# Which keys of a fused attention and feed-forward kernel the SP queue loads, and a new written-out order of its operations

## The chip, the cores and the metric

The kernel runs on one core of a Trainium2 chip. A core has five engines that run side by side and wait for one another by semaphores: TensorE (PE in the profile; PEld is its loading of weights), VectorE (DVE), ScalarE (ACT), GpSimd (POOL) and SyncE (SP), and 16 DMA engines that move data between the main memory (DRAM) and the on-chip memory. A DMA is issued by an instruction in the queue of SP, ACT or POOL. The metric is the device time of one execution in microseconds (us).

## The reference

```python
# attention: q, k, v are [4 batches, 8 heads, 768 tokens, 64] float32
scores = (q @ k.transpose) / sqrt(64)
keep   = (key position < 4) | (0 <= token - key position < 128)     # 4 sinks and a window of 128
a      = softmax(where(keep, scores, -1e9))
x      = (a @ v), heads side by side: [3072 tokens, 512]
# feed-forward: w_in [512, 2048], w_out [2048, 512]
h      = x @ w_in
out    = (h * sigmoid(1.702 * h)) @ w_out                            # [3072, 512] float32
```

## The kernel before

**Tiling.** The 3072 tokens are 24 blocks of 128 tokens, 6 for each batch. The list `ORDER` (0, 6, 12, 18, 1, 2, 3, ...) says in which order the blocks are worked on; the text calls the place of a block in it its position p0 to p23. Positions 0 to 3 are the first blocks of the four batches (block 0, 6, 12, 18). Because the window is as long as a block, a block needs the keys and values of itself and of the block before it, and the four sinks. Two positions make a group: g0 is p0 and p1, up to g11.

**Attention of one block.** Its q and its k are loaded as fp16 into a buffer `qkn` (a ring of 4, one for each group). They are transposed into `qkt`: for p0 to p7 by TensorE (`t_qk`, w0 for q and w1 for k, lines 420 and 427) with a copy out of PSUM by ACT or DVE (`copy_qk`), later by a transposing DMA of SP (line 455). Then come the scores (`scores`, line 503; `masks`, line 495, for p0 to p3), on DVE the packing of both halves (549), the maximum (559, 570 to 579) and its subtraction (600, 624), on ACT the exponential (639), the transposition of the weights `a` into `at` (TensorE, line 679, up to p5; then a DMA of SP, line 704), two selections on POOL (642, 646), the product with the values (`values`, lines 731, 737, 741), the normalization on DVE (`norm`, 748 and 749) into `xn`, and the transposition of `xn` into `xt` (TensorE, line 767, up to p5; then one DMA of SP for each group, line 780).

**Feed-forward of one group.** 8 operations `first` (line 802) make `h` transposed, ACT or ACT with DVE apply the gate into `gt` (832, 816, 823), and 8 operations `second` (line 856; t0 and t1 for the two blocks, n0 to n3 for quarters of the contraction) make the output, which is copied out of PSUM (`osb`, 377 or 381) and stored (874). `first` and `second` of an earlier group stand in TensorE's queue between the attention of later blocks. PSUM buffers of the ring `mm` (3) serve the transpositions, `first` and `second`.

**Loads.** POOL issues the loads that change the type from fp32 to fp16 on the way: q and k of p0 to p3 in large pieces (line 299), the others in small ones (306), the values (277), four parts of w_in (315, here i0 to i3) and four of w_out (324, o0 to o3). One load goes another way: the blocks named by `CFG["hw"]` are loaded as fp32 by SP into a tile `raw`, and one of three engines rounds it into `qkn`:

```python
got = plan.add({SP: 0.45, ACT: 0.6}, -120 + n, 0, lambda e, ...: by(e).dma_start(raw, src), ...)      # line 284
return plan.add({DVE: 0.42, ACT: 0.6, POOL: 0.8}, -110 + n, 0, round16, deps=[got], take=[buf])       # line 295
```

**The order.** Every operation is put on a list by `plan.add` and has its number there. What is issued, in which order and on which engine, is read from the string `SEQUENCE` alone: `37s` is operation 37 on SP, and the letters p, a, d, t, s stand for PE, ACT, DVE, POOL and SP. The costs given to `plan.add` (0.57 and the like) are not used by `run`:

```python
for word in SEQUENCE.split():                                                                         # line 142
    op = self.ops[int(word[:-1])]
    op.on = {"p": PE, "a": ACT, "d": DVE, "t": POOL, "s": SP}[word[-1]]
```

Each engine works its own operations off in this order, and a later one never passes an earlier one of the same engine or queue. Which buffer of a ring an operation gets follows from the order too.

Of the kernel before, what the change touches and what calls it, by code (L numbers as in the profile page):

```python
# [27 lines left out]
PE, ACT, DVE, POOL, SP = "PE", "ACT", "DVE", "POOL", "SP"  # L28
# [30 lines left out]
126p 8d 125a 26t 149p 109d 127a 147p 21t 129p 110d 148a 130p 23t 111d 150a 2d 112a 131d 33t 114p 113a 133d 172p 116p  # L59
115a 105t 132d 152p 135a 117d 120p 30t 173a 134d 170p 118p 137p 121d 29t 136a 153p 119d 139p 138a 122p 171a 141p  # L60
154d 24t 140a 175p 155d 143p 156d 123a 176p 151t 157d 144d 481p 142d 158a 34t 484p 482a 177d 145p 9d 159a 483d 146a
160p 180d 485a 161d 27t 182a 487p 486d 488a 178d 128t 493p 162p 489d 494a 163d 28t 495d 490p 179d 166p 164p 40t 491a
167d 478p 183p 492d 39t 181a 165d 479a 32t 184d 499p 185p 187p 480d 36t 500a 186d 195p 193p 189p 501d 43t 194a 188d
496p 196a 217p 31t 190d 215p 168p 497a 197p 169a 498d 191p 218a 216a 199d 514p 198p 42t 192a 508p 200d 201d 518p
515a 519a 509p 35t 202d 239p 203d 237p 48t 219p 220p 240a 238a 54t 502p 221d 503p 222d 520p 204a 223d 46t 504p 224d
225d 510p 5d 241p 93s 226a 49t 1s 511p 45t 512d 505p 242p 521a 73t 516p 243d 506a 44t 517a 524p 205p 244d 41t 525a
245d 528p 206d 247d 529a 522p 253p 255p 246d 523a 254d 530p 256d 61t 208p 227p 209d 257p 97d 207t 248a 531p 270s
230p 228a 259d 210t 231a 532p 258p 260d 211p 229t 261d 526p 249s 212d 263d 232t 533p 233p 52t 262d 527a 536p 55t
234d 213p 214d 57t 537p 271p 51t 264a 534a 538p 235p 273d 265s 236a 539p 272p 250t 274d 540a 548p 275d 53t 277d 552p
62t 276d 550p 549a 283p 296s 553a 554p 284p 285d 555a 266t 542p 94s 551a 286d 251p 59t 287d 544p 47t 252d 545a 289d  # L70
546p 58t 543a 267p 547a 50t 288d 558p 268d 564p 297p 278a 269s 556p 513s 298p 299d 565p 279s 300d 559p 541s 557a
301d 507s 98t 566p 95s 302d 60t 303d 578p 290a 567p 309p 568d 304a 291s 560p 311d 576p 280t 305s 579a 312d 561p 577a
281p 562a 310p 570p 282d 322s 313d 571a 572p 292t 574p 314d 315d 535s 575a 65t 580p 293p 581a 66t 573a 584p 294d
585a 586p 306t 295s 592p 74t 587p 316a 90t 582p 64t 307p 317s 69t 593p 308d 583a 67t 588p 323p 63t 604p 70t 325d
605a 589p 324p 56t 590a 326d 594p 79t 327d 612p 72t 328d 613a 600p 335p 601a 595p 318t 337d 329d 596a 606p 174t 607a
348s 598p 338d 602p 336p 603a 339d 608p 341d 599a 319p 609a 340d 620p 320d 614p 330a 610p 321s 615p 342a 361p 621p
343s 362p 611a 363d 563s 622p 591s 364d 616p 365d 331s 638p 366d 639a 617p 367d 374s 618a 623p 344t 349p 75t 632p
597s 351d 569s 633a 628p 350p 624a 352d 634p 332t 353d 345p 635a 355d 84t 629a 630p 346d 68t 631a 636p 88t 626p 85t
333p 627a 637a 91t 640p 334d 78t 641a 648p 354d 99t 347s 642p 81t 649p 375p 76t 356a 650p 377d 368a 643p 376p 357s
378d 651p 379d 369s 644p 380d 668p 625s 652d 387p 619s 645p 389d 669a 656p 400s 646d 657a 660p 358t 390d 381d 658p  # L80
659a 662p 370t 359p 663a 83t 654p 360d 77t 655a 664p 388p 661a 71t 371p 391d 665a 82t 666p 372d 670p 392d 393d 382a
373s 676p 401p 394a 383s 671p 403d 677p 402p 667a 395s 404d 678p 405d 647s 407d 672p 96s 679p 406d 680d 673p 413p
384t 674d 684p 408a 415d 696p 385p 409s 414p 416d 396t 685a 686p 386d 687a 426s 690p 397p 691a 697a 692p 398d 693a
688p 417d 419d 410t 689a 399s 682p 86t 418d 411p 683a 80t 694p 412d 87t 695a 698p 427p 100t 699p 429d 420a 710p 430d
700p 428p 421s 431d 701p 681s 711a 702a 716p 432d 724p 452s 439p 725a 717a 675s 718p 703s 441d 433d 719a 712p 422t
713a 714p 442d 440p 715a 443d 720p 423p 721a 732p 424d 704p 444d 434a 445d 722p 733p 446a 435s 705p 653s 734p 723a
425s 465p 706p 466p 447s 467d 726p 468d 735p 436t 469d 471d 736a 707p 437p 708a 470d 709s 727p 438d 746p 448t 747a
742p 89t 449p 743a 92t 728p 450d 738p 472a 451s 729p 737s 453p 730d 744p 739a 473s 455d 745a 752p 456d 750p 751a
740p 454p 741a 457d 772p 459d 753a 773a 748p 458d 749a 778p 474t 779a 760p 768p 761p 460a 770p 762p 461s 475p 771a
763p 769a 476d 764a 766p 767a 774p 775a 776p 777a 782p 462t 783p 780p 781a 788p 784p 463p 789p 464d 754p 477s 790p  # L90
731s 785p 786d 791p 792d 755p 796p 797a 756p 802p 803a 757p 758d 806p 759s 807a 808p 793s 809a 787s 794p 765s 795a
798p 799a 800p 822p 801a 804p 823p 805a 810p 824p 811p 825p 826d 816p 827a 812p 817p 813p 818p 828p 814a 819p 829p
815s 830p 820d 831p 832a 821s 833a
"""


# [69 lines left out]
def kernel(  # L166
# [224 lines left out]
    o_qkt, o_ks, o_own_s, o_x = {}, {}, {}, {}  # L391

    for p, b in enumerate(ORDER):
        bb, r = divmod(b, 6)
        g, i = divmod(p, 2)
        K0 = 8 * p
# [5 lines left out]
        if p in CFG["tq"]:  # L402
# [36 lines left out]
            for w in range(2):  # L439
                a = plan.add(  # L440
                    PE, K0 - 48 + w, 0.43 if p in CFG["big"] else 0.24, lambda w=w, f=t_qk: f(w), deps=[ld["qk"[w] + str(b)], o_const],
                    take=[tps[w]], give=[qkn[g]],
# [4 lines left out]
                        lambda e, b=b, w=w, f=copy_qk: f(e, w),  # L447
                        deps=[a], take=[qkt[g]], give=[tps[w]],
# [60 lines left out]
        if r == 0:  # L509
            s_msk = plan.add(  # L510
                PE, K0 - 41, 0.45, lambda own=half, f=masks: f(own), deps=[o_const] + (o_qkt[b] if p else []), take=uniq(owns),
                slack=slack["s"],
            )
            s_own = plan.add(
                PE, K0 - 40, 0.46, lambda b=b, own=half, f=scores: f(own, b),
                deps=o_qkt[b] + [s_msk], give=[qkt[g]], use=uniq(owns),
            )
        else:

            def both(b=b, own=half, prv=prv, f=scores):  # L520
# [12 lines left out]

            s_snk = plan.add(PE, K0 - 40, 0.1, sinks, deps=([s_own] if p >= CFG['steady'] else []) + o_qkt[b] + [o_ks[bb]], take=[snk], give=[qkt[g]], slack=slack["s"])
# [9 lines left out]
        for lo, hi in parts:  # L544
            packed = s_own
            if r > 0:

                def pack(lo=lo, hi=hi, own=half, prv=prv):
# [13 lines left out]
                    deps=[packed], use=uniq(owns[lo:hi]),  # L562
# [22 lines left out]
        if nb:  # L585
# [6 lines left out]
                deps=[top] + (mx if nb == 2 or not first else mx[1:]),  # L592
# [58 lines left out]
        if r > 0 and nb == 0 and len(subs) == 1:  # L651
            e_all = plan.add(
                ACT, K0 - 36, 1.02, lambda f=exp: f(0, 1056), deps=[subs[0][2], sub_snk] + ready[0],
                take=[a16], give=[e32], table="exp", slack=slack["e"],
            )
            ready, e_snk = [[e_all], [e_all]], None
        else:
            for lo, hi, o_sub in subs:
                o_e = plan.add(
                    ACT, K0 - 36 + 0.1 * lo, 0.1 + 0.43 * (hi - lo), lambda lo=lo, hi=hi, f=exp: f(512 * lo, 512 * hi),  # L660
                    deps=[o_sub] + ready[lo], take=[a16], give=[e32], table="exp",
# [4 lines left out]
            if r > 0:  # L666
                e_snk = plan.add(
                    ACT, K0 - 36, 0.15, lambda f=exp: f(1024, 1056),
                    deps=[sub_snk] + ready[0][:1], take=[a16], give=[e32], table="exp",
                )  # L670
        o_at = [None, None]
        if p in CFG["ta"]:
            for l in range(2):
# [11 lines left out]
                def ev_a(e, at=at, tpa=tpa, l=l, n=len(chunks)):  # L685
# [76 lines left out]
        if p in CFG["tx"]:  # L762
            tpx = ps("mm", (P, 4, P), FP16, f"tx{b}")

            def t_x(xn=xn, tpx=tpx, i=i):
# [7 lines left out]
                deps=[o_tx], take=[xt[g]], give=[tpx],  # L773
# [3 lines left out]
        else:  # L777
# [5 lines left out]
                deps=norms0 + norms, take=[xt[g]], give=[xn], xfer=1.28, post=0.75,  # L783
# [3 lines left out]
    for g in range(NG):  # L787
# [5 lines left out]
        for u in range(8):  # L793
# [18 lines left out]
            if 2 * g + (u // 4 if split else 0) in CFG["tanh"]:  # L812
# [6 lines left out]
                    deps=[o_h], take=[th], table="exp",  # L819
# [101 lines left out]
```

## Time and profile before

| what | value |
|---|---|
| median of 3 runs | 227.39 us (227.13 to 227.76) |
| the profiled execution's own time | 228.47 us |
| its span | 226.8 us |
| busy share of the span | PE 94%, PEld 67%, ACT 62%, DVE 58%, POOL 51% |
| bytes moved | 32.47 MB, 143 GB/s in the mean |
| granted TensorE clock | 1.00 of full speed throughout |

The profiled execution took 1.08 us more than the median of the runs; 1.67 us of its time lie outside the span.
How to read it: the busy share of PE counts matmuls from start to modelled end, so it shows where PE had nothing to do rather than how well it worked. A line of a view names the engine, the line of the kernel, output and input by name, and in square brackets the idle time before it and what ended that.

### The profile page before, as it was taken

Reading aid. Unit: us, or ns where it says so; the run is one execution under the profiler, and the core shown is the slowest. Engines: PE = TensorE matmul, PEld = TensorE weight load, DVE = VectorE, ACT = ScalarE, POOL = GpSimd, SP = SyncE. Lnnn points to the kernel's source line nnn. Section 1 sums busy time; section 2 is a strip of 40 time slices with the busy share of each in tenths; the row PEclk is TensorE's granted clock in tenths of the full one; section 3 lists DMA queues with packets and bytes.
Section 4 is the critical chain, followed back from the end, with each engine's and each line's share of the span. In section 5 each row is a group of like instructions: output and inputs, shape, how many; then the busy total and the mean of one; then the engine's idle time right before and its main releaser. Section 6 shows DMA issues by size and latency. Waiting matters only on the chain.

```text
span 226.8 us, 5647 instructions
## 1 busy us (share of the span) xinstructions
PE 214.0 (94%) x2378; PEld 151.5 (67%) x2378; DVE 132.2 (58%) x237; ACT 141.4 (62%) x201; POOL 115.1 (51%) x138
## 2 busy tenths in 40 slices
PE   0998999999999999999999999999999999999994
PEld 0567875776774595685695695695764777755863
DVE  2599897688797561674656937965746463112100
ACT  3688696897669648358259258768583678711521
POOL 8963844769785399730895580763304612300000
PEclk9999999999999999999999999999999999999999
DMA  6999999999999999994999999379908780203402
GB/s 132 170 204 191 175 192 193 157 144 143 131 149 158 260 186 141 141 167 92 249 185 146 256 106 174 91 168 86 271 8 191 85 155 3 52 0 95 166 31 81
DMA packets 123512, 32.47 MB, mean 143 GB/s; under 512 B 114880, under 2 KB 120416, under 8 KB 123488
## 3 DMA queue, kind: packets, MB, share of 16 engines
q0 software_dynamic: 71792, 13.51, 73.6%
q1 hardware_dynamic: 51408, 18.49, 37.8%
q8 instruction: 18, 0.29, 0.5%
q10 hardware_dynamic: 288, 0.13, 0.2%
q14 instruction: 6, 0.05, 0.1%
HBM read 27.46 MB, written 6.29 MB: 149 GB/s over the span
## 4 chain that ended last, share of the span: by engine, by line
PE 75%; DMA 15%; POOL 4%; DVE 3%; issue 1%; ACT 0%; POOLq 0%
PE mm L856 34%; PE mm L802 30%; DMA w_in<-in_moe_w_in_dram 6%; DMA xt<-xn 5%; DMA qkn<-in_q_dram 4%; PE own L503 2%; PE av L737 2%; PE av L741 2%; PE av L731 2%; PE prv L503 2%; POOL qkn L299 2%; POOL w_in L315 1%; DVE xn L749 1%; POOL v L277 1%; PE snk L532 1%
## 5 line engine op out<-in xcount | busy, mean ns | idle before, releaser
L802 PE MATMUL mm<-xt,w_in 128*128 128x256 f16 (+1 forms) x896 | 93.3, 258 | 1.6 <-DMA xt<-xn 1.0
L856 PE MATMUL mm<-w_out,gt 128*128 128x512 f16 (+2 forms) x416 | 92.0, 363 | 0.0
L802 PEld LDWEIGHTS <-w_in 128*128 128x128 f16 x896 | 75.5, 98 | 14.9 <-DMA xt<-xn 1.2
L832 ACT ACTIVATE gt<-mm 128x512 f16<-128x512 f32 x88 | 50.6, 597 | 53.4 <-PE mm L802 51.5
L856 PEld LDWEIGHTS <-gt 128*128 128x128 f16 x416 | 37.0, 98 | 32.3
L642 POOL TENSOR_SCALAR_AFFINE_SELECT atp<-at 128x1024 f16<-128x1024 f16 (+1 forms) x22 | 22.2, 1010 | 64.6 <-DMA at<-a 64.5
L549 DVE COPY_PREDICATED own<-consts,prv 128x1024 f32<-128x1024 uint16 x20 | 24.5, 1226 | 21.4 <-PE prv L503 21.4
L559 DVE TENSOR_REDUCE mx<-own 128x8 f32<-128x1024 f32 (+1 forms) x28 | 29.8, 1068 | 6.0 <-PE own L503 5.4
L600 DVE TENSOR_TENSOR e<-own,mx 128x1024 f32<-128x1024 f32 (+1 forms) x26 | 28.4, 1095 | 0.6
L639 ACT ACTIVATE a<-e 128x1056 f16<-128x1056 f32 (+1 forms) x26 | 25.1, 980 | 1.9 <-DVE e L624 1.3
L646 POOL TENSOR_SCALAR_AFFINE_SELECT at<-at 128x1024 f16<-128x1024 f16 (+1 forms) x22 | 22.5, 1024 | 1.5
L277 POOL DMA_DIRECT2D v<-in_v_dram x24 | 21.5, 901 | 3.0 <-DMA w_out<-in_moe_w_out_dram 1.9
L748 DVE RECIPROCAL rcp<-av 128x8 f32<-128x8 f32 (+1 forms) x25 | 5.0, 199 | 30.7 <-PE av L741 30.3
L306 POOL DMA_DIRECT2D qkn<-in_k_dram x20 | 17.8, 895 | 8.0 <-DMA w_out<-in_moe_w_out_dram 3.1
L639 ACT ACT_TABLE_LOAD x14 | 18.0, 1283 | 2.4 <-issue 2.2
L832 ACT ACT_TABLE_LOAD x15 | 19.2, 1283 | 0.3
L377 DVE COPY osb<-mm 128x512 f32<-128x512 f32 (+2 forms) x11 | 6.9, 629 | 21.4 <-PE mm L856 20.9
L306 POOL DMA_DIRECT2D qkn<-in_q_dram x20 | 18.0, 900 | 1.2 <-DMA w_out<-in_moe_w_out_dram 1.0
L737 PE MATMUL av<-v,at 128*128 128x65 f16 x180 | 16.1, 194 | 0.5 <-DMA v<-in_v_dram 0.5
L749 DVE TENSOR_TENSOR xn<-av,rcp 128x512 f16<-128x512 f32 (+1 forms) x25 | 16.0, 638 | 0.9
L737 PEld LDWEIGHTS <-at 128*128 128x128 f16 x192 | 14.0, 98 | 2.8 <-DVE at L377 0.7
L381 ACT COPY osb<-mm 128x512 f32<-128x512 f32 (+1 forms) x13 | 7.3, 559 | 12.4 <-PE mm L856 12.4
(65 smaller groups left out, 174.9 us busy)
## 6 DMA issues: line engine op xcount, KB each, us to landing
out_dram<-osb SPq DMA_DIRECT2D x23, 256.0 KB, 2.9
qkn<-in_q_dram POOLq DMA_DIRECT2D x24, 128.0 KB, 6.2
v<-in_v_dram POOLq DMA_DIRECT2D x24, 128.0 KB, 5.2
qkn<-in_k_dram POOLq DMA_DIRECT2D x23, 128.0 KB, 5.8
w_in<-in_moe_w_in_dram POOLq DMA_DIRECT2D x4, 512.0 KB, 10.5
w_out<-in_moe_w_out_dram POOLq DMA_DIRECT2D x4, 512.0 KB, 10.8
at<-a SPq DMA_TRANSPOSE x18, 3.5
raw_k<-in_k_dram SPq DMA_DIRECT2D x1, 256.0 KB
```

The costliest lines, as they stand in the source:

```text
L277: return sw(key, 0.88, lambda b=b, x=2: nc.gpsimd.dma_start(v65[:, b, :, 0:D], src), 0.88 if pair < 4 else 0.95, deps=[z_1], after=after)
L306: key, 0.88, lambda b=b, w=w, i=i: nc.gpsimd.dma_start(buf()[:, i, w], src), 0.88 if pair < 4 else 0.95,
L549: nc.vector.copy_predicated(out=own(lo, hi).rearrange("p l j s -> p (l j) s"), mask=later.unsqueeze(1).to_broadcast((P, 4 * (hi - lo), P)) ...
L559: lambda lo=lo, hi=hi, own=half, small=small: nc.vector.tensor_reduce(out=small[:, lo:hi], in_=own(lo, hi), axis=AX.X, op=ALU.max),
L600: nc.vector.tensor_tensor(out=e32()[:, 512 * lo : 512 * hi].rearrange("p (l j s) -> p l j s", j=4, s=P), in0=own(lo, hi), in1=small[:, lo: ...
L639: nc.scalar.activation(out=a16()[:, lo:hi], in_=e32()[:, lo:hi], func=AF.Exp, scale=scale)
L642: nc.gpsimd.affine_select(out=atp()[:, lo : lo + n], in_=at()[:, lo : lo + n], pattern=[[0, n], [-1, P]], compare_op=ALU.is_gt, fill=0.0, ...
L646: nc.gpsimd.affine_select(out=at()[:, lo : lo + n], in_=at()[:, lo : lo + n], pattern=[[0, n], [1, P]], compare_op=ALU.is_ge, fill=0.0, ba ...
L737: nc.tensor.matmul(acc[:, j], at()[:, c], v65[:, b, h], start=(r == 0), stop=(r == 0))
L802: nc.tensor.matmul(ht()[:, n], w_in16[:, c, bass.ts(f, P)], xt[g]()[:, tok, c], start=(c == 0), stop=(c == 3))
L832: lambda fs=fs, cols=cols, gt=gt, ht=ht: nc.scalar.activation(out=gt()[:, fs[0] : fs[-1] + 1, cols], in_=ht(), func=AF.Gelu_apprx_sigmoid),
L856: nc.tensor.matmul(po(), gt()[:, F, bass.ts(t, P)], w_out16[:, F, cols], start=(F == 0), stop=(F == NF - 1))
```

## The change

Three settings and the sequence differ. `hw` names the keys of p1 (block 6) in place of those of p0 (block 0), so SP's fp32 load and the operation 38 that rounds it now belong to p1's keys, and POOL loads q and k of p0 itself; the list of loads has k0 where it had k1. `actq` permits the load of the constants on ACT's queue (the sequence has it on SP in both kernels, `0s`). A cost of 0.57 becomes 0.65. The sequence is another one. The few words that name the change say that DVE rounds; in the sequence the rounding is `38t`, on POOL (before: `38a`, on ACT). Cut to its core:

```diff
-    hw=['k0'],
+    hw=['k1'],
-    actq=0,
+    actq=1,
-    loads="q0 q1 k1 q2 k2 q3 k3 v0 v1 i0 i1 v2 v3 i2 i3 o0 o1 q4 k4 v4 o2 q5 k5 v5 o3".split(),
+    loads="q0 k0 q1 q2 k2 q3 k3 v0 v1 i0 i1 v2 v3 i2 i3 o0 o1 q4 k4 v4 o2 q5 k5 v5 o3".split(),
 SEQUENCE = """
-37s 6d 7d 0s 12t 4d 16t 15t 3d 10d 13t 11a 14t 38a 17t 18t 103p 20t 104a 101p 19t 102a 106p 22t 107p 25t 124p 108d
...
+37s 4d 0s 10d 13t 11a 12t 3d 16t 2d 14t 38t 18t 15t 106p 20t 103p 17t 104a 101p 19t 126p 102d 6d 22t 8d 127a 107p 7d
...
-                PE, K0 - 40, 0.57, both, deps=o_qkt[b] + o_qkt[b - 1], take=uniq(owns) + [prv],
+                PE, K0 - 40, 0.65, both, deps=o_qkt[b] + o_qkt[b - 1], take=uniq(owns) + [prv],
```

What the two sequences say engine by engine, at the places that matter (q0 is the load of p0's q, and so on; before, then after):

| queue and place | before | after |
|---|---|---|
| POOL, start | q0 k2 q2 q1 k1 q3 k3 v1 v0 i1 i2 i3 i0 v2 q5 (sinks p0) k4 q4 v3 ... | k0 q0 k2 q1 (rounding of k1) k3 q2 v1 q3 v0 i1 i2 i3 i0 v2 k4 v3 q5 q4 ... |
| PE, start | k0, q0, masks p0, scores p0, q1, k1, k2, q2, masks p1, scores p1 | masks p0, k0, q0, k1, scores p0, q1, k2, k3, q2, masks p1, scores p1 |
| PE, from the end of the values of p7 to the first `first` of g3 | 5 `second`, 1 `first`, scores p10, sinks p10 | 8 `second`, 1 `first`, scores p10 and p11, sinks p10 |
| PE, values of p9 to `first` of g4 | 2 `first`, 5 `second`, values p10, scores p12 | 2 `first`, 4 `second`, values p10 |
| PE, values of p17 to `first` of g8 | 4 `first`, 2 `second`, values p18, scores p20 | 5 `first`, 1 `second`, values p18, sinks p19 |
| PE, values of p19 to `first` of g9 | 1 `first`, 10 `second`, values p20, scores and sinks p23 | 1 `first`, 5 `second`, scores p23, two sinks |
| SP, around the `xt` transposition of g8 | `at` p18, `qkt` g10, `xt` g8 | `qkt` g10, `at` p18, `xt` g8 |
| SP, from the `xt` transposition of g11 to the end | 6 full stores, then 1 of the last block's 3 parts (the other two are ACT's) | 5 full stores, with that of p18 as the last of them, behind that of p22; then 2 parts (the last is ACT's) |

Besides, the copy of p0's transposed q goes from ACT to DVE, that of the second half of p0's weights from DVE to ACT, and some 16 later copies and small products change between DVE, ACT and POOL.

More of the change, by code (lines that the diff above doesn't have):

```diff
@@ L63 @@
[L63 to L92, printed above, removed]
@@ new lines @@
+524p 253p 206a 255p 525a 256d 522p 254a 207t 246d 523a 530p 227p 54t 208p 228d 257p 209a 97t 270s 531p 258p 259d
+210t 532p 230p 248a 260d 211p 229t 231a 526p 249s 212d 232t 261d 533p 60t 233p 262d 527a 52t 536p 213p 234d 263d
+214d 51t 537p 55t 271p 235p 272p 58t 264a 538p 273d 236a 62t 539p 534a 274d 265s 151t 540a 548p 275d 94s 552p 276d
+550p 250t 549a 296s 283p 551a 65t 554p 285d 555a 541s 542p 251p 543a 286d 277d 266t 544p 284p 252d 545a 57t 546p
+287d 553a 267p 47t 547a 288d 289d 558p 64t 268d 556p 50t 297p 278a 174t 269s 564p 290a 299d 559p 298p 279s 300d 565p
@@ new lines @@
+557a 301d 513s 560p 95s 302d 566p 98d 303d 291s 561p 535s 309p 562d 567p 311d 280t 304a 578p 568d 53t 580p 305s 312d
+570p 507s 579a 281p 571a 292t 572p 310p 282d 322s 573a 313d 576p 581a 574p 314d 315d 293p 575a 577a 582p 294d 586p
+306t 295s 584p 316a 70t 587p 67t 307p 317s 585a 59t 588p 583a 308d 63t 592p 89t 608p 79t 609a 589p 323p 56t 590d
+600p 68t 325d 601a 604p 66t 324p 99d 605a 593p 82t 326d 606p 69t 327d 329d 607a 594p 72t 328d 602p 603a 598p 318t
+335p 599a 612p 337d 613a 595p 348s 338d 614p 336p 596d 319p 339d 591s 330a 620p 320d 341d 615p 340d 321s 610p 616p
@@ new lines @@
+342a 621p 361p 343s 611a 569s 622p 362p 363d 617p 331s 563s 364d 638p 618d 639a 623p 365d 367d 374s 624a 632p 344t
+366d 633a 628p 78t 625s 349p 629a 634p 351d 626p 332t 345p 627a 352d 350p 81t 635a 630p 346d 71t 631a 353d 640p 76t
+636p 354d 75t 355d 333p 637a 77t 648p 334d 642p 356a 375p 347s 649p 368a 377d 357s 643p 378d 650p 376p 641a 379d
+644p 400s 381d 651p 380d 658p 369s 387p 659a 96s 652a 358t 645p 653s 389d 90t 656p 597s 646d 92t 660p 359p 661a 654p
+360d 370t 655a 668p 388p 390d 84t 669a 664p 391d 85t 665a 662p 392d 657a 393d 91t 371p 663a 74t 666p 372d 670p 401p
@@ new lines @@
+373s 382a 676p 394a 403d 383s 671p 402p 404d 677p 667a 405d 395s 672p 647s 406d 678p 407d 673p 426s 413p 674d 684p
+408a 384t 415d 679p 385p 685a 409s 696p 396t 386d 697a 692p 680a 416d 397p 693a 686p 398d 690p 691a 399s 682p 414p
+410t 683a 694p 417d 687a 83t 688p 418d 419d 80t 411p 689a 695a 87t 698p 412d 100t 724p 88t 699p 420a 427p 700p 428p
+421s 429d 725a 701p 430d 702a 710p 431d 703s 711a 712p 675s 432d 713a 433d 718p 719a 720p 452s 422t 439p 86t 714p
+441d 715a 716p 423p 717a 442d 440p 721a 443d 732p 424d 722p 445d 733p 434a 444d 425s 704p 465p 435s 723a 734p 467d
@@ new lines @@
+705p 466p 468d 746p 446a 469d 471d 706p 447s 470d 735p 747a 436t 736d 707p 708d 738p 437p 472a 726p 438d 473s 742p
+739a 448t 743a 727p 449p 744p 450d 745a 750p 453p 751a 451s 619s 728p 737s 455d 681s 474t 740p 741a 456d 729p 752p
+730d 753a 748p 770p 454p 771a 457d 766p 459d 767a 778p 458d 475p 779a 749a 760p 476d 780p 761p 460a 762p 461s 772p
+781a 763p 773a 764a 768p 765s 769a 774p 709s 775a 776p 777a 754p 462t 788p 782p 463p 755p 464d 783p 477s 789p 756p
+784p 757p 758d 785p 786d 790p 787s 806p 807a 802p 803a 791p 792d 796p 793s 797a 808p 731s 809a 794p 795a 798p 799a
@@ L94 @@
+800p 801a 810p 804p 805a 811p 816p 812p 813p 817p 822p 814a 818p 823p 815s 819p 759s 828p 824p 820d 829p 825p 830p
+821s 826d 831p 832a 827s 833a
 """
```

13 lines of the change are left out of this document (8 added, 5 removed).

## The prediction

> **What bounds the kernel now.** I read the page first, for which engine is busy and which work the last chain runs through.
>
> ```profile
> PE 214.0 (94%) x2378; PEld 151.5 (67%) x2378; DVE 132.2 (58%) x237; ACT 141.4 (62%) x201; POOL 115.1 (51%) x138
> ...
> PE 75%; DMA 15%; POOL 4%; DVE 3%; issue 1%; ACT 0%; POOLq 0%
> ```
>
> PE is busy for 214.0 of 226.8 us, and three quarters of the chain are PE. The change neither adds nor takes a matmul, so it can move the time only by PE's idle time: the 5.5 us before the first matmul, the gaps, and the 3.1 us behind the last one. So I read next what PE waited for, first in the view of waits from 0 to 45 us (four lines), then from 35 to 227 us (the last line). The columns are total us, times, longest us.
>
> ```profile
> PE tq L420 <- DMA consts<-cconst: 5.5, 1, 5.5
> PE mm L802 <- DMA w_in<-in_moe_w_in_dram: 0.5, 1, 0.5
> PE av L737 <- DMA v<-in_v_dram: 0.5, 1, 0.5
> PE mm L427 <- DMA qkn<-in_q_dram: 0.4, 1, 0.4
> ...
> PE mm L802 <- DMA xt<-xn: 1.0, 2, 0.7
> ```
>
> Two kinds remain. Up to 35 us PE waits for loads, each time for one that POOL issued. Behind that, in 190 us, it waits for 1.0 us in two places, both for the `xt` transposition of a group. The timeline of PE gives the places of the early ones, and the chain of waits shows that the last of them is a DMA of 9.9 us behind an issue of POOL:
>
> ```profile
> 22.42 1.07 PE L802 MATMUL mm<-xt,w_in 128*128 128x128 f16 x16 [0.48 <-DMA w_in<-in_moe_w_in_dram]
> 26.70 0.30 PE L737 MATMUL av<-v,at 128*128 128x65 f16 x4 [0.46 <-DMA v<-in_v_dram]
> 34.43 0.40 PE L427 MATMUL mm<-consts,qkn 128*128 128x128 f16 x4 [0.41 <-DMA qkn<-in_q_dram]
> ...
> 24.47 9.91 DMA qkn<-in_q_dram
> ```
>
> At 34.43 us PE stands still until the q of p6 lands, whatever it did before. Up to that point both sequences let PE do the same operations, and POOL issues the same loads. So the start is set by the stream of POOL's loads: if the stream is x later, PE is x later at 34.4 us, and nothing behind it gives that back by itself.
>
> **The stream of loads: a stop in POOL's queue.** POOL's timeline, and what its first loads took from issue to landing (first load; third and fourth; fifth):
>
> ```profile
> 1.32 0.68 POOL L299 DMA_DIRECT2D qkn<-in_q_dram  x1 [0.81 <-POOLq L902]
> ...
> 2.52 1.05 POOL L299 DMA_DIRECT2D qkn<-in_q_dram  x2
> 3.52 0.56 POOL L299 DMA_DIRECT2D qkn<-in_k_dram  x1
> ...
> 6.80 3.07 POOL L315 DMA_DIRECT2D w_in<-in_moe_w_in_dram  x4
> ...
> DMA to landing us min/median/max: 3.8/3.8/3.8
> ...
> DMA to landing us min/median/max: 4.0/4.1/4.1
> ...
> DMA to landing us min/median/max: 4.3/4.3/4.3
> ```
>
> The first load lands at 5.1, the fourth (issued at 3.0) at 7.1, the fifth at 7.8: one lands every 0.7 us, though POOL issues one every 0.55, so from the start the DMA engines set the pace. In the new sequence POOL's fifth instruction is the rounding of k1, which must wait until SP's fp32 load has landed; k3, q2, both values and all of w_in are queued behind it. When that load lands, and what rounding on POOL may take, ACT's and POOL's rows say:
>
> ```profile
> 4.47 0.62 ACT L291 CAST qkn<-raw_k 128x512 f16<-128x512 f32 x1 [1.22 <-DMA raw_k<-in_k_dram]
> ...
> 48.06 0.63 POOL L642 TENSOR_SCALAR_AFFINE_SELECT atp<-at 128x512 f16<-128x512 f16 x1
> 57.08 1.12 POOL L642 TENSOR_SCALAR_AFFINE_SELECT atp<-at 128x1024 f16<-128x1024 f16 x1
> ```
>
> The load stays first in SP's queue, so POOL starts rounding at 4.5. No row shows a cast on POOL. Its nearest rows are selections: 0.63 us for as many elements, 1.12 for as many bytes read; I take 0.63. The next load is then issued at 5.1 instead of 3.52. If it takes the 3.8 us of the first load it lands at 8.9, where the pace of 0.7 us behind the fourth would have had it at 7.8: the stream is 1.1 late, 1.6 with a rounding of 1.12. The other end is nothing: when POOL stops at 3.5, the engines have work until shortly before 7.1, and the first load shared the engines with SP's, so the new one may be quicker. I take **x = +0.7 us**, in the middle and nearer to the end whose row is of the same kind. The Trainium skill, "GPSIMD Engine Reference", section 3.1, gives 769 ns for 512 elements in a measured loop of POOL; POOL's row of 0.63 for as many elements is shorter. With the page's figure x would be some 0.1 more, an estimate from that page.
>
> The rest of the start I cost at nothing, under cover of this stream.
>
> ```profile
> 6.14 0.58 ACT L381 CAST qk<-tq 128x512 f16<-128x512 f32 x1 [1.05 <-PE tq L420]
> 7.42 0.61 PE L503 MATMUL own<-qk 64*128 64x128 f16 x8
> ...
> 16.70 1.96 PE L802 MATMUL mm<-xt,w_in 128*128 128x128 f16 x32
> ```
>
> ACT loses the cast (0.62) and one copy (0.58) and gets another copy; DVE gets that copy of q. The scores of p0 move a little behind 7.4, since `masks` now stand ahead of the transpositions. But from the first `first` at 16.7 (two of them in the 1.96) to the wait that ends at 22.42 PE has 5.7 us and only four `first`, some 3.9 us by that row, and three short transpositions to do. So p0's chain may be about a microsecond late before PE notices; beyond that the price is what it is late.
>
> The settings `actq` and 0.65 issue nothing, since the order is written out.
>
> **The waits for `xt`.** Both places in the chain of waits, with SP's rows from its timeline between them (the two of 145.56 and 147.04), and the time of all nine transpositions to landing:
>
> ```profile
> 67.69 0.70 DVE xn L749
> ...
> 68.40 5.51 DMA xt<-xn
> ...
> 145.56 1.31 SPq L704 DMA_TRANSPOSE at<-a  x1
> 147.04 1.60 SPq L455 DMA_TRANSPOSE qkt<-qkn  x1
> ...
> 150.14 0.69 DVE xn L749
> 150.86 5.85 DMA xt<-xn
> ...
> DMA to landing us min/median/max: 2.8/4.1/5.8
> ```
>
> PE's wait at 73.96 was 0.69 us of the 1.0, that at 156.75 the other 0.30 (both in PE's timeline); behind them, from the chain of waits, what PE's operations take:
>
> ```profile
> 73.96 0.72 PE L802 MATMUL mm<-xt,w_in 128*128 128x256 f16 x5 [0.69 <-DMA xt<-xn]
> 156.75 0.49 PE L802 MATMUL mm<-xt,w_in 128*128 128x256 f16 x3 [0.30 <-DMA xt<-xn]
> ...
> 101.27 0.11 PE av L731
> ...
> 101.98 1.73 PE mm L856 x8
> 103.70 0.87 PE mm L802 x8
> ...
> 105.44 0.33 PE own L503 x8
> 105.77 0.22 PE prv L503 x8
> ```
>
> A `second` takes 0.865 us (1.73 for two), a `first` 0.87, scores 0.55 (0.33 + 0.22), the values 0.7 (101.27 to 101.98). In group 3 the new sequence puts three more `second` and the scores of p11 ahead of the first `first`: 3.1 us of PE work, where 0.69 were missing. Its DVE and SP orders leading to this `xt` are nearly the old ones. **That wait goes: -0.69 us.** Next late there would be nothing for 2.4 us.
>
> In group 8 the new sequence has 0.45 us less work (a `first` and small sinks more, a `second` and the scores less). Against that, SP now issues `qkt` of g10 ahead of `at` of p18 and no longer 3.8 us ahead of this `xt`. Its 5.85 us are the longest of nine; the two longest are 5.5 and 5.8, the median is 4.1. If it falls to the median, it lands 1.7 earlier, more than 0.45 + 0.30. **I take that wait as gone: -0.30 us.**
>
> Two other groups come near. By the same rows group 4 keeps 2 x 0.87 + 4 x 0.865 + 0.7 for the values of p10 = 5.9 us (it had 7.3), group 9 1 x 0.87 + 5 x 0.865 + 0.55 + 0.2 = 5.9 (it had 10.8), and group 8 has 6.0. What they need is about 1.0 us from the end of the values to SP's issue (DVE's 0.69, and some 0.3 that I allow for the reciprocal ahead of it and the hand-over) and the landing: 5.1 with the median, 6.8 with the longest. At the median none waits. I allow **+0.5 us**, one wait of the size of the mean of the two old ones, for what a new order of 800 operations brings in such places; its ends are 0 and the rival below.
>
> **The end.** SP issues a part of the last block that ACT issued before, and one full store late. The last chain stays PE, ACT's copy, ACT's DMA:
>
> ```profile
> 223.71 0.27 ACT osb L381
> ...
> 224.00 0.34 ACTq L874 DMA_DIRECT2D out_dram<-osb  x1
> ```
>
> I take 0; at most it is one issue more in the way, +0.34, and as much less if SP's earlier parts were what ended last.
>
> **Sum.** +0.7 - 0.69 - 0.30 + 0.5 + 0 = +0.2 us. The profiled execution's span of 226.8 would be 227.0, its own time of 228.47 some 228.7; that execution was 1.1 us above the median, so I add the 0.2 to the median of 227.39: **227.6 us**. About 0.3%, 0.68 us, is what a measurement of this kernel can tell from no change, so the forecast is "the same".
>
> **Rivals.** *Slower: the transpositions of `xt` land late in the tight groups.* If those of groups 4, 8 and 9 take the 5.5 to 5.85 us that two of nine took, each finds 5.9 to 6.0 us of PE work where 6.5 to 6.9 are needed, and PE stands 0.6 to 0.9 us in each. It decides from a landing of about 4.9 us on. For it: two of nine took that long, the one of 150.86 3.8 us behind a `qkt`. Against it: the median of 4.1. With two such waits instead of my 0.5: 227.39 + 0.7 - 0.69 + 2 x 0.8 = 229.0 us; with one and x at 1.1, 228.6.
>
> *Faster: the stop in POOL's queue is hidden.* If the next load's data is at the engines when the fourth's is through, x is near 0, and if the new order brings no wait: 227.39 - 0.69 - 0.30 = 226.4 us. For it: four loads are in flight at the stop. Against it: the 3.8 us of the first load.
>
> *The change doesn't do what its words say.* With DVE rounding, POOL would not stop and x were 0, with my 0.5 kept: 226.9 us. The sequence has the rounding on POOL, so I give this no chance of its own.
>
> **Chances and range.** The forecast, within 0.68 us of 227.39, has 0.36; the slower rival, with a longer stop of POOL as its helper, 0.36; the faster one 0.28. The range of 8 in 10 goes from the faster rival's 226.4 to the slower one's 229.0; the forecast's own is 226.7 to 228.1.
>
> **What would show it.** Right, if POOL's fifth load is issued at about 5.1 us behind a cast of 0.6, if the parts of w_in are issued about 1.6 later than at 6.80 and the wait for the q and k of p6 ends at about 35.1 instead of 34.43, and if no wait for `xt` stands before the first `first` of group 3. Wrong, if the cast runs on another engine, if the wait at 34.43 ends no later, if the landing of `xt` in groups 4, 8 or 9 leaves PE idle by more than 0.5 us, or if PE waits after 35 us for something that isn't `xt`.

## The result and the profile after

The changed kernel took 229.5 us in the median of 7 runs (228.91 to 230.87), the kernel before 227.49 us in 7 runs beside it (227.13 to 228.4). The ratio is 1.0084, with a 95% interval of 1.0057 to 1.011. That is slower, outside the predicted range (226.4 to 229.0) and outside the forecast of "the same".

The profiled execution of the changed kernel took 228.91 us, with a span of 227.2 (before: 228.47 and 226.8). The page's busy line and its chain:

```profile
PE 214.4 (94%) x2378; PEld 151.9 (67%) x2378; DVE 137.0 (60%) x239; ACT 142.7 (63%) x201; POOL 114.3 (50%) x138
...
PE 78%; DMA 14%; POOL 4%; DVE 3%; issue 1%; ACT 0%; POOLq 0%
```

PE has the same 2378 matmuls and is busy about as long as before (214.4 and 214.0). The work is the same, so I look again at where PE waits. The two profiled executions' spans are only 0.4 us apart, of the 2.0 between the medians, so they can show where time is lost, but not all of it. The view of waits of the changed kernel, from 0 to 45 us (first four lines) and from 35 us to the end (the rest):

```profile
PE own L495 <- DMA consts<-cconst: 5.1, 1, 5.1
PE mm L802 <- DMA w_in<-in_moe_w_in_dram: 1.8, 2, 1.4
PE mm L767 <- DVE xn L749: 0.8, 2, 0.4
PE mm L427 <- DMA qkn<-in_k_dram: 0.4, 1, 0.4
...
PE own L503 <- DVE e L600: 0.2, 1, 0.2
PE mm L802 <- DMA xt<-xn: 0.2, 1, 0.2
```

Before, PE waited 0.5 us for `w_in` at the start and 1.0 us for `xt` behind it. Now it is 1.8 and 0.2: better behind 36 us and worse ahead of it. The sum of the waits for `w_in` is not the loss, though: the kernel before has 1.7 us of them in a second profile (before_p1, below), and its wait for p6 ends at 34.53, against 34.43 in the first. What counts is when that wait ends. POOL's timeline shows where the start begins to be late:

```profile
4.39 0.61 POOL L293 CAST qkn<-raw_k 128x512 f16<-128x512 f32 x1 [0.83 <-DMA raw_k<-in_k_dram]
4.95 0.52 POOL L299 DMA_DIRECT2D qkn<-in_k_dram  x1
5.45 0.53 POOL L299 DMA_DIRECT2D qkn<-in_q_dram  x1
5.95 0.93 POOL L277 DMA_DIRECT2D v<-in_v_dram  x1
6.85 0.56 POOL L299 DMA_DIRECT2D qkn<-in_q_dram  x1
7.36 0.94 POOL L277 DMA_DIRECT2D v<-in_v_dram  x1
8.26 0.80 POOL L315 DMA_DIRECT2D w_in<-in_moe_w_in_dram  x1
```

POOL stands idle for 0.83 us, rounds for 0.61, and then issues without a gap up to `w_in` at 8.26, where it was 6.80 before: 1.46 us later. In this pair of profiles the landing doesn't give that back: the first part of `w_in` (its row in the view of the tile) took the same time in both kernels.

```profile
DMA to landing us min/median/max: 7.8/7.8/7.8
```

But the first profile of the kernel before is the quickest of the seven without a stop of POOL. Two others (before_p1, then e1_p2, which is the new order with the rounding on ACT):

```profile
DMA to landing us min/median/max: 8.5/8.5/8.5
...
DMA to landing us min/median/max: 9.0/9.0/9.0
```

Over all of them (table below), the four profiles with the changed kernel's stop (its three and e9_pool_store) issue this part 1.3 us later than the seven without, and it takes 7.8 us in the mean to land instead of 8.3: it lands 0.8 later.

What hangs on `w_in` is seen in POOL's timeline from 22 us on, first before, then after:

```profile
22.66 0.74 POOL L324 DMA_DIRECT2D w_out<-in_moe_w_out_dram  x1 [1.45 <-DMA w_in<-in_moe_w_in_dram]
23.59 0.89 POOL L306 DMA_DIRECT2D qkn<-in_k_dram  x1 [0.19 <-issue]
24.47 0.88 POOL L306 DMA_DIRECT2D qkn<-in_q_dram  x1
```

```profile
24.42 0.74 POOL L324 DMA_DIRECT2D w_out<-in_moe_w_out_dram  x1 [2.27 <-DMA w_in<-in_moe_w_in_dram]
25.36 0.88 POOL L306 DMA_DIRECT2D qkn<-in_q_dram  x1 [0.21 <-issue]
26.24 0.46 POOL L470 COPY ksb<-qk 64x16 f16<-64x16 f16 x2
26.64 0.87 POOL L306 DMA_DIRECT2D qkn<-in_k_dram  x1
```

POOL waits until `w_in` has landed before it issues the next part of `w_out`, and the second of the two loads of p6 comes behind that. So the chain to PE's wait for p6 is POOL's stop, `w_in`, `w_out`'s issue, p6's load. The issue of `w_out` is 1.76 us later. Then the new order adds something of its own: two copies of sink keys (`ksb`), which the old order did at 11.55, 15.84 and 20.78 us, the last two pairs just ahead of waits for `w_in`, now stand between p6's two loads, and the second load is issued 0.40 us later for them. Together its issue is 2.17 us later (26.64 for 24.47). It then lands 0.58 us quicker (9.33 for 9.91 in the chains of waits). So the copies' 0.40 us are not lost: the two loads of p6 land 0.8 us apart here (25.36 + 9.8 and 26.64 + 9.33) and 0.9 before (23.59 + 9.9 and 24.47 + 9.91). PE's wait ends 1.59 us later than at 34.43:

```profile
36.02 0.40 PE L427 MATMUL mm<-consts,qkn 128*128 128x128 f16 x4 [0.42 <-DMA qkn<-in_k_dram]
```

### The profile page after: what moved, and what is told of

It reads as the page before. It is cut to its first block, busy times and chain, and to the rows that moved or that the text cites. A ratio compares the mean times of both kernels' runs of the same rounds, so it can differ in the third digit from the quotient of the medians.

```text
span 227.2 us, 5653 instructions
## 1 busy us (share of the span) xinstructions
PE 214.4 (94%) x2378; PEld 151.9 (67%) x2378; DVE 137.0 (60%) x239; ACT 142.7 (63%) x201; POOL 114.3 (50%) x138
## 4 chain that ended last, share of the span: by engine, by line
PE 78%; DMA 14%; POOL 4%; DVE 3%; issue 1%; ACT 0%; POOLq 0%
PE mm L856 34%; PE mm L802 32%; DMA w_in<-in_moe_w_in_dram 6%; DMA qkn<-in_k_dram 4%; PE own L503 3%; DMA xt<-xn 2%; PE av L737 2%; PE av L741 2%; PE prv L503 2%; PE av L731 2%; DMA raw_k<-in_k_dram 2%; POOL w_in L315 1%; POOL v L277 1%; POOL qkn L299 1%; PE snk L532 1%
## 5 line engine op out<-in xcount | busy, mean ns | idle before, releaser
L856 PE MATMUL mm<-w_out,gt 128*128 128x512 f16 (+1 forms) x416 | 91.8, 363 | 0.0
L377 DVE COPY osb<-mm 128x512 f32<-128x512 f32 (+2 forms) x15 | 9.7, 645 | 23.3 <-PE mm L856 21.2
L741 PE MATMUL av<-v,atp 128*128 128x65 f16 x160 | 14.7, 193 | 0.0
```

The costliest lines, as they stand in the source:

```text
L856: nc.tensor.matmul(po(), gt()[:, F, bass.ts(t, P)], w_out16[:, F, cols], start=(F == 0), stop=(F == NF - 1))
```

## The experiments

The theories. **A:** POOL's stop behind four loads makes the whole load stream late, and PE with it; that is the loss. **B:** the new order itself costs, wherever the rounding is done. **C:** the new order of the start costs (p0's pair by POOL, the masks first). **D** (later D'): waits for `xt` in the tight groups (group 4 above all) take back what the order gains. Ratios are to the kernel before on the same chip, with 95% intervals; single runs of one kernel scatter by 0.4 to 0.9 us (standard deviation), so a difference of 0.2% between two kernels is not told apart by 12 runs each.

**The change again (after_again).** No edit.

> The changed kernel once more, beside which the next ones stand. All theories: 0.7 to 1.0% above the kernel before, the wait for the keys of p6 ending near 36.0 us.

229.1 us, 1.0046 [1.002, 1.0071], span 227.0. The wait for p6 ends at 35.87. The ratio is less than the 0.7 to 1.0% expected. No wait for `xt` stands behind the start at all, and the kernel is still slower: D can't be the whole of it.

**The rounding moved off POOL, in the new order (e1_act, e2_dve).**

```diff
-... 2d 14t 38t 18t 15t 106p ...      (changed kernel: POOL rounds)
+... 2d 14t 38a 18t 15t 106p ...      (e1_act; e2_dve has 38d)
```

> The changed kernel with the rounding of p1's keys on ACT (38a) in place of POOL, so POOL's queue does not stop; everything else as in the changed kernel. Theory A (POOL's stop makes the whole stream of loads late, and PE with it): the first part of w_in is issued near 6.8 us instead of 8.26 and lands near 14.6 instead of 16.1, the wait for p6's keys ends near 34.5, and the time falls by about 1.5 us against the changed kernel, to within 0.3% of the kernel before. Theory B (the cost is in the new order behind 35 us): the issue moves as in A, but the time falls by less than 0.5 us. Theory C (the cost is in the new order of the start, p0's pair by POOL and the masks first): the first matmuls of the first layer stay late, and the time falls by less than 0.5 us.

> The changed kernel with the rounding on DVE (38d), as the words of the change say. Theory A: as on ACT, about 1.5 us less than the changed kernel; the two agree within 0.3 us, since both engines are idle from 3 to 6.7 us. Theories B and C: less than 0.5 us.

e1_act: 228.16 us, 0.9994 [0.997, 1.0017]. e2_dve: 228.05 us, 0.9989 [0.9965, 1.0013]. Both are 0.9 to 1.1 us below the changed kernel on this chip (A expected 1.5, B and C less than 0.5) and level with the kernel before. The load of `w_in` is back where it was; POOL's timeline of e2_dve, and PE's at the wait for p6:

```profile
5.92 0.99 POOL L277 DMA_DIRECT2D v<-in_v_dram  x1
6.81 2.41 POOL L315 DMA_DIRECT2D w_in<-in_moe_w_in_dram  x3
...
35.18 0.40 PE L427 MATMUL mm<-consts,qkn 128*128 128x128 f16 x4 [0.42 <-DMA qkn<-in_k_dram]
```

So B and C fall as the loss: without the stop the new order shows no loss against the old one. It shows no gain either, and e1_act shows one place where it gives back. PE's timeline of e1_act at group 4, and the time to landing of that transposition from the view of the tile:

```profile
90.52 1.05 PE L802 MATMUL mm<-xt,w_in 128*128 128x256 f16 x8 [1.43 <-DMA xt<-xn]
...
DMA to landing us min/median/max: 6.2/6.2/6.2
```

**The stop alone, in the old order (e3_before_pool).**

```diff
-... 13t 11a 14t 38a 17t 18t 103p ...      (kernel before: ACT rounds)
+... 13t 11a 14t 38t 17t 18t 103p ...
```

> The kernel before with its one rounding (p0's keys) moved from ACT to POOL (38t), so POOL stops behind five issued loads instead of four; order and loads as before. Theory A: the sixth load is issued near 5.0 instead of 4.02, w_in about 1.0 later than 6.80, and the time is 0.7 to 1.1 us above the kernel before. Theories B and C: within 0.3 us of the kernel before.

229.12 us, 1.0033 [1.0007, 1.006]: slower, with nothing else changed. In the old order the stop comes one load later. POOL's timeline, PE's at the wait for p6 and PE's at group 3:

```profile
4.45 0.61 POOL L293 CAST qkn<-raw_k 128x512 f16<-128x512 f32 x1 [0.36 <-DMA raw_k<-in_k_dram]
...
7.78 1.53 POOL L315 DMA_DIRECT2D w_in<-in_moe_w_in_dram  x2
...
35.24 0.40 PE L427 MATMUL mm<-consts,qkn 128*128 128x128 f16 x4 [0.20 <-DMA qkn<-in_q_dram]
...
74.28 1.05 PE L802 MATMUL mm<-xt,w_in 128*128 128x256 f16 x8 [0.45 <-DMA xt<-xn]
```

`w_in` is 0.98 us late, the wait for p6 ends 0.81 late, and the ratio of 1.0033 is 0.75 us.

**The kernel before once more (before_p1).** No edit; the question was whether its waits for `xt` were those of one execution.

> The kernel before, one more profiled execution. Theory A says that the two waits for xt in its first profile (0.69 in group 3, 0.30 in group 8) belong to that execution, which took 1.1 us more than the median: here they are shorter together by 0.5 us or more if the time is near the median, and the wait for p6's queries ends between 34.3 and 34.8. If they are there again at a time near the median, the new order did gain them, and something else of that size must have been lost.

One run, 228.27 us; span 226.5; p6's wait ends at 34.53. The wait in group 3 is there again, and longer:

```profile
74.23 1.05 PE L802 MATMUL mm<-xt,w_in 128*128 128x256 f16 x8 [1.10 <-DMA xt<-xn]
```

So the expectation failed: the waits sum to 1.10 us against 0.99, in an execution 0.3 us under the median beside it. The wait in group 3 belongs to the old order; it stood in all three of its profiles (0.69, 1.10, 0.45). That in group 8 (0.30) was in one only.

**The stop doubled (e4_twice).** POOL does the rounding twice.

```diff
 # in round16, line 293
+                    if e == POOL:
+                        nc.gpsimd.tensor_copy(out=dst, in_=src)
```

> The changed kernel with the rounding done twice on POOL, so the stop is 0.6 us longer; nothing else. Theory A: w_in is issued near 8.8 instead of 8.25, the wait for p6's keys ends near 36.5, and the time is 0.4 to 0.7 us above the changed kernel (1.007 of the kernel before, where the changed one had 1.005). Theories B and C: no change against the changed kernel.

230.21 us, 1.0105 [1.0069, 1.014]. POOL's timeline and PE's (lines are two higher here):

```profile
4.28 0.61 POOL L293 CAST qkn<-raw_k 128x512 f16<-128x512 f32 x1 [0.71 <-DMA raw_k<-in_k_dram]
4.95 0.61 POOL L295 CAST qkn<-raw_k 128x512 f16<-128x512 f32 x1
...
8.82 2.28 POOL L317 DMA_DIRECT2D w_in<-in_moe_w_in_dram  x3
...
36.75 0.40 PE L429 MATMUL mm<-consts,qkn 128*128 128x128 f16 x4 [0.38 <-DMA qkn<-in_k_dram]
```

Another 0.6 us on POOL makes `w_in` 0.56 later and PE 0.73 later than in the changed kernel's first profile: here the longer stop passes on fully. The ratio, of 6 runs, is above the changed kernel's three (1.0046 to 1.0084), but its interval overlaps theirs, so the runs alone don't show that it adds.

**The stop two loads later (e5_later).**

```diff
-... 14t 38t 18t 15t 106p ...
+... 14t 18t 15t 38t 106p ...
```

> The changed kernel with the rounding still on POOL, but two loads later in its queue (behind k3 and q2). Theory A: POOL has issued six loads when SP's load lands and hardly waits, so only the 0.6 us of the rounding itself is left; w_in is issued near 7.4, the wait for p6's keys ends near 34.5 to 35.0, and the time is 0.6 to 1.0 us below the changed kernel, within 0.2% of the kernel before. If the work on POOL counts and not the wait, it is 0.3 us below the changed kernel at most.

228.24 us, 1.0013 [0.9986, 1.0041]: most of the loss is gone with the same cast on the same engine.

```profile
4.81 0.61 POOL L293 CAST qkn<-raw_k 128x512 f16<-128x512 f32 x1 [0.22 <-DMA raw_k<-in_k_dram]
...
7.67 1.53 POOL L315 DMA_DIRECT2D w_in<-in_moe_w_in_dram  x2
...
34.73 0.40 PE L427 MATMUL mm<-consts,qkn 128*128 128x128 f16 x4 [0.19 <-DMA qkn<-in_k_dram]
```

`w_in` is issued 0.86 us later than in e2_dve, yet PE's wait ends no later (34.73 against 35.18). Its first part takes 7.5 us to land, at 15.2, as early as in the new order without a stop (14.8 to 15.8). The stop is shorter here, since POOL waits only 0.22 us for SP's load instead of 0.83; what is left of it is hidden. Six loads are issued ahead of it, four in the changed kernel. That fits the cover the prediction hoped for, two loads further on; one profile shows it, and the shorter stop and the longer cover were not tried apart.

**More work ahead of group 4's `first` (e7_room).** e2_dve with a `second` and the scores of p12 moved there, to fill the wait that D names.

```diff
-... 592p 89t 608p 79t 609a 589p 323p 56t ...
+... 592p 89t 79t 589p 323p 608p 609a 56t ...
```

> The changed kernel with the rounding on DVE, and in group 4 one second and the scores of p12 put ahead of the first matmuls that need xt, so PE has 7.3 us of work there as in the kernel before instead of 5.9. Theory D (without the stop the new order loses at group 4 what it gains at groups 3 and 8; its profile with ACT had 1.43 us of waiting there, that with DVE none): the time falls by 0.2 to 0.7 us below that with DVE alone, 0.997 to 0.998 of the kernel before. If group 4 does not matter: 0.999 as with DVE alone.

228.54 us, 1.0012 [0.9985, 1.0039]. No wait for `xt`, though it landed 5.5 us after its issue, but another in its place, for the gate of the `first` that was moved back:

```profile
92.77 1.91 PE L802 MATMUL mm<-xt,w_in 128*128 128x256 f16 x16 [0.69 <-ACT gt L832]
```

That expectation failed: here the room was taken from the next place.

**A store of SP moved behind group 4's `xt` (e8_store, with e1_act repeated as e1_p2, and e9_pool_store).** In the new order SP has a store and a long `qkt` ahead of that `xt`. SP's timeline of the kernel before, then of the changed kernel:

```profile
78.80 1.61 SPq L455 DMA_TRANSPOSE qkt<-qkn  x1
80.46 0.67 SPq L874 DMA_DIRECT2D out_dram<-osb  x1
85.27 1.25 SPq L780 DMA_TRANSPOSE xt<-xn  x1
```

```profile
79.58 0.58 SPq L874 DMA_DIRECT2D out_dram<-osb  x1
80.32 4.07 SPq L455 DMA_TRANSPOSE qkt<-qkn  x1
85.62 1.24 SPq L780 DMA_TRANSPOSE xt<-xn  x1
```

```diff
-... 570p 507s 579a 281p ... 306t 295s 584p ...      (295s is xt of g4, 507s the store)
+... 570p 579a 281p ... 306t 295s 507s 584p ...      (e8_store: in e1_act; e9_pool_store: in the changed kernel)
```

> The new order with the rounding on ACT, and one full output store of SP (507s) moved from ahead of the qkt transposition of g6 to behind the xt transposition of g4. Theory D' (in the new order that store and the long qkt of g6 hold up xt of g4, and this is where the order gives back its gain behind p6): qkt of g6 is issued about 0.6 us earlier, xt of g4 lands at or before 90.0 us instead of 90.4, PE's wait before the first `first` of g4 falls from 1.43 us to under 0.9, and the time is 0.9965 to 0.998 of before. Rival (the landing time of xt g4 is not set by that store; what the order gains is small and spread, and lost in several places): the wait stays over 1.1 us or another appears, and the time stays at 0.999 to 1.001 of before.

> The new order with the rounding on ACT, once more, beside the last run on the same chip. Theory A: 0.997 to 1.001 of before, 0.4 to 0.8% below the changed kernel on this chip, w_in issued at 6.8 us. If the wait of 1.43 us before the first `first` of g4 belongs to the order (theory D'), it comes back with 1.0 to 1.6 us; if it belonged to that one execution, it is under 0.5.

> The changed kernel as it is, a third profile and a third ratio, since the two so far (1.0084 and 1.0046) lie apart. Theory A (POOL's stop makes w_in's issue 1.5 us late, PE's wait for the q and k of p6 ends 1.4 to 1.6 us later than before): w_in issued at 8.2 to 8.3 us, that wait ends at 35.9 to 36.1, the ratio is 1.004 to 1.008. Rival (the loss varies from execution to execution in waits behind 40 us): the wait ends as late, but PE's waits behind 40 us sum to over 1 us in this profile.

On one chip, 12 runs each: e8_store 227.73 us, 0.9971 [0.9949, 0.9992]; e1_p2 227.62 us, 0.9988 [0.9962, 1.0015]; the changed kernel a third time 229.8 us, 1.0068 [1.0037, 1.0099]. So with the rounding on ACT the new order is 2.2 us faster here, more than the 0.4 to 0.8% expected. In after_p3 the start is late, by 1.2 us (35.70, where A said 35.9 to 36.1), and group 4 waits as well, so that the waits behind 40 us sum to 1.3 us: the rival's sign is there too (PE's timeline):

```profile
35.70 0.40 PE L427 MATMUL mm<-consts,qkn 128*128 128x128 f16 x4 [0.42 <-DMA qkn<-in_k_dram]
...
91.42 1.05 PE L802 MATMUL mm<-xt,w_in 128*128 128x256 f16 x8 [1.10 <-DMA xt<-xn]
```

In e1_p2 the wait of 1.43 us is not there: `xt` landed in 4.6 us. So that wait comes and goes from execution to execution. In e8_store `qkt` is issued in 2.60 us, and the first `first` of group 4 starts without a wait (SP's timeline, then PE's):

```profile
78.71 2.60 SPq L455 DMA_TRANSPOSE qkt<-qkn  x1
84.69 1.23 SPq L780 DMA_TRANSPOSE xt<-xn  x1
85.97 0.58 SPq L874 DMA_DIRECT2D out_dram<-osb  x1
...
89.41 1.04 PE L802 MATMUL mm<-xt,w_in 128*128 128x256 f16 x8
```

So `xt` landed in at most 4.7 us there. But since e1_p2 has no wait either, and the two medians are 0.1 us apart, the store's worth in time is not shown.

> The changed kernel with the rounding left on POOL, and only the output store 507s of SP moved from ahead of the qkt transposition of g6 to behind the xt transposition of g4. Two profiles of three of the changed kernel show a wait before the first `first` of g4 (0.16 and 1.10 us). Theory A with D' (the late stream costs the start, the store costs group 4, and both add): w_in is still issued at 8.2 us, the wait for the q and k of p6 still ends at 35.7 to 36.0, no wait for xt stands in group 4, and the time is 1.001 to 1.005 of before, 0.2 to 0.5% below the changed kernel's three ratios of 1.0046 to 1.0084. Rival (the store has no part in the loss): a wait in group 4 of 0.3 us or more, or a ratio of 1.006 or more.

229.36 us, 1.0055 [1.0028, 1.0083]. No wait for `xt` in group 4, as expected; the time is above the expected band and within the scatter of the changed kernel's three ratios. PE's wait for p6 ends at 36.89, a microsecond later than expected: the second load of p6 took 10.3 us to land (9.3 in the changed kernel), and a part of `w_out` ahead of it 11.4 (10.3). Moving the store did not take the loss away, and the start is late as before.

e8_store is the only version whose interval lies below 1. But e1_p2 beside it has the same median, so what is shown of a gain over the kernel before is small (0.1 to 0.5%) and can't be put down to the store.

## Why the prediction was wrong

The profiles put side by side. "`w_in`" is the issue of its first part and the time from there to its landing, "start" is the end of PE's wait for p6 (in e1_act it comes without a wait), "rest" the span minus it, "xt" the waits behind it.

| kernel | rounding | `w_in` issued | to landing | start | rest | xt waits |
|---|---|---|---|---|---|---|
| before, before_p1 | ACT, old order | 6.80, 6.79 | 7.8, 8.5 | 34.43, 34.53 | 192.4, 192.0 | g3 0.69 and g8 0.30; g3 1.10 |
| e3_before_pool | POOL, old order | 7.78 | 7.9 | 35.24 | 191.5 | g3 0.45 |
| changed, three profiles | POOL, new order | 8.26, 8.24, 8.16 | 7.8, 7.9, 7.3 | 36.02, 35.87, 35.70 | 191.2, 191.1, 192.3 | g4 0.16; none; g4 1.10 |
| e9_pool_store | POOL, new order | 8.21 | 8.2 | 36.89 | 191.0 | none |
| e4_twice | POOL twice | 8.82 | 7.6 | 36.75 | 191.3 | none |
| e1_act, e1_p2 | ACT, new order | 6.82, 6.81 | 8.0, 9.0 | 34.4, 34.99 | 192.7, 191.2 | g4 1.43; none |
| e8_store | ACT, new order | 7.14 | 8.3 | 34.99 | 191.1 | none |
| e2_dve, e7_room | DVE, new order | 6.81, 7.19 | 8.1, 8.3 | 35.18, 35.06 | 191.0, 191.8 | none; none |
| e5_later | POOL, later | 7.67 | 7.5 | 34.73 | 191.8 | g4 0.34 |

**The start: +0.7 us forecast, 1.4 measured.** This is the step that failed. The prediction took x, the price of POOL's stop, at +0.7 and the rest of the start at nothing. The start is 1.38 us later in the mean of the changed kernel's three profiles (35.86 against 34.48 of before's two). The five profiles of the new order without a stop (e1_act, e1_p2, e8_store, e2_dve, e7_room) lie between, at 34.92 in the mean. So some 0.9 us are the stop's and some 0.4 the new order's.

**x: right mechanism, too small.** The stop cost 0.9 us at PE in the profiles, and more in the runs: without it the new order was 0.9 to 1.1 us faster on one chip and 2.1 to 2.2 on another. The rounding began at 4.39 and took 0.61, as said, and the next load was issued at 4.95 (forecast 5.1). The prediction put the price on the landing of that load and let the loads behind it be as late. That load was not late: it landed 3.7 us after its issue, at 8.65, where the five profiles without a stop have it at 8.1 to 9.1. Nor was the one behind it; from the third on they were, by 0.5 to 0.6 us in the mean. So the reading "from the start the DMA engines set the pace" held as long as loads were queued ahead of them; then POOL, which issued without a gap at 0.52 to 0.94 us for each load, seems to have set it.

The last load ahead of `w_in` landed at 12.3 to 12.6 us with the stop (the changed kernel's profiles and e9_pool_store) and at 11.3 to 12.0 without, and the first part of `w_in` 0.7 later than in the same order without a stop (16.0 against 15.3). Its issue was 1.3 later, so about half was made up on the way. That the stream came out 0.7 late, as forecast, is partly luck, since the load that gave the figure was on time. What makes 0.9 at PE out of it, and up to 2.2 in the runs, isn't settled.

The Trainium skill, "DMA: Bandwidth & Descriptors", section "Issuing engines are not separate DMA queues", says that the time an issuing engine spends on starting transfers is usually small beside the transfers themselves. The trace agrees for the loads behind the stop: 0.52 to 0.94 us to issue, 3.7 to 4.9 to landing. Still, of a stop of 1.44 us in the issuing queue some 0.9 reached PE.

**"The rest of the start I cost at nothing": missed, some +0.4 us, cause open.** Without a stop the new order's start ends at 34.4 to 35.2, the old order's at 34.43 and 34.53. The two copies of sink keys between p6's two loads, which the table of queues in front of the prediction let one expect, are not shown to cost anything, since the two loads land no further apart than before. The lateness stands ahead of them: the last part of `w_in` lands at 23.0 to 23.6 us in the five profiles, and at 22.4 and 22.7 in the kernel before. Why, no run shows.

**The price of the rounding: right.** 0.63 was taken, 0.61 measured; that of the bytes read (1.12) was not the right neighbour. The Trainium skill, "GPSIMD Engine Reference", section 3.1, has 769 ns for 512 elements; the cast, with as many in each partition, took 609.

**The wait in group 3, -0.69: right.** No profile of the new order shows it, all three of the old order do.

**The wait in group 8, -0.30: right by its reason, small in worth.** No profile of the new order has it. With `qkt` of g10 moved away from just ahead of it, this transposition landed 2.7 us after its issue in the changed kernel (the view of the tile, 145 to 158 us), against 5.8 before and 5.0 in before_p1; 4.1 was the prediction's figure:

```profile
DMA to landing us min/median/max: 2.7/2.7/2.7
```

But before_p1 has no wait there, so the 0.30 were one execution's.

**The allowance of +0.5 for a new wait: right place, and the threshold held.** The slower rival named group 4 and said that it decides from a landing of about 4.9 us on. Of the new order's profiles, those with a landing of 4.3, 4.4, 4.6 and 4.9 (e4_twice, after_again, e1_p2, e2_dve) have no wait, and those with 5.0, 5.2, 6.0 and 6.2 wait 0.16, 0.34, 1.10 and 1.43. It happens in some executions, 0.4 us in the mean of the changed kernel's three. In the new order groups 8 and 9 never waited: their landings were 2.7.

**The end, 0:** no run shows a loss there.

**The sum.** With the measured start, 1.38 instead of 0.7, and the rest of 191.5 in the mean instead of 192.2 (-0.7, forecast -0.49), the profiles give +0.7 us. The runs give more: 1.0046, 1.0068 and 1.0084 are +1.05, +1.55 and +1.9 us. In numbers the difference lies in which executions were profiled: the changed kernel's (228.91, 228.75, 229.68) were 0.1 to 0.6 us under their medians, the first one of the kernel before 1.0 above its median (228.47 and 227.49), the second 0.3 under. The prediction took its two waits from that first, slow execution and subtracted them from a median; whether a median execution has them, no profile shows. What the slower executions of the changed kernel do differently isn't settled: waits in group 4 and for `w_out` that vary between profiles are of that size, but no profile caught one. What is shown without that gap: the rounding off POOL takes the loss away (0.9994, 0.9989, 0.9988), and POOL's stop alone brings one in the old order (1.0033). Of the prediction's signs of being right, the issue of `w_in` and the wait in group 3 came; the end of the wait for p6 at about 35.1 did not. Of the rivals, the slower one came true in sign, by its "helper", the longer stop, more than by its own mechanism; the faster one (the stop is hidden) is what e5_later shows for a stop two loads later.

## What to carry to other kernels

An instruction that waits or computes in a queue that also issues loads delays the issue of every load behind it, not only of the next one, and the next one can be on time while those behind it are late. How much of the delay arrives is another matter: here 1.3 us at the issue of `w_in` became 0.7 at its landing and 0.9 at the consumer, and with two more loads ahead of the cast, where the issue was 0.7 late, nothing was left (one profile). So follow the landings, not the issues, down to the last load on which something waits, and look at several executions: the landing of one and the same load, issued 6.8 to 7.2 us into the run, lay between 14.6 and 15.8 us without any stop, so a single pair of profiles can be off by a microsecond. Likewise, don't charge a small operation between two loads until their landings have moved apart.

## What the runs showed of the hardware

GpSimd's cast of 128x512 from fp32 to fp16 takes 0.61 us, as long as ACT's (0.62) for the same tile. A load whose issue was delayed by POOL's stop landed sooner after it: the first part of `w_in` in 7.3 to 8.2 us, against 7.8 to 9.0 without a stop. The landing of the `xt` transposition varied with its place: 2.7 us for several groups of the new order, 4.3 to 6.2 for group 4. There it stood behind a `qkt` whose issue took 3.4 to 4.1 us in eight of the nine profiles that have a store just ahead of it (4.07 in the changed kernel, 2.16 in e4_twice), 2.6 and 1.8 with the store moved (e8_store, e9_pool_store), and 1.5 to 1.6 in the old order, where the store comes behind it and group 4's `xt` landed in 4.1 to 4.8. What sets the landing isn't shown.
